# A two-layer attention and MLP kernel: loads of the ramp put later, ninth score blocks in shared units, a fourth bank pair for scores, and an instruction order found anew

## The chip, the core and the metric

The kernel runs on one core of a Trainium2 chip. The core has five engines with instruction streams of their own: TensorE (PE, with its weight loads shown apart as PEld), VectorE (DVE), ScalarE (ACT), GpSimd (POOL) and SyncE (SP), which here issues the DMAs. The metric is the device time of one execution in microseconds. The kernel before was run three times.

## The reference, cut to what matters

```python
def _A_ref(x, wqkv, wo):                 # B, S, D = 1, 2048, 576
    H = 32; Dh = D // H; W = 256         # 32 heads of 18
    q, k, v = split(x @ wqkv)
    scores = q k^T * Dh ** -0.5          # per head
    mask = (i - j >= 0) & (i - j < W)    # causal, sliding window of 256
    p = softmax(where(mask, scores, -1e9))
    return (p v) @ wo

def _B_ref(x, w1, b1, w2, b2):           # F = 4608
    y = layernorm(x)
    return gelu(y @ w1 + b1) @ w2 + b2

x = x + _A_ref(layernorm(x), wqkv, wo)
x = x + _B_ref(layernorm(x), w1, b1, w2, b2)
x = x + _A_ref(layernorm(x), wqkv, wo)
x = x + _B_ref(layernorm(x), w1, b1, w2, b2)
```

Both layers use the same weights. All tensors are bf16; the kernel keeps x in fp32.

## The kernel before, in words

**Tiles and chunks.** The 2048 rows are 16 tiles of 128. A chunk k is four tiles (512 rows) of one layer, so there are eight chunks; 0 and 4 are the first ones of their layers ("edge chunks"). A chunk goes through these stages, whose names the planner uses:
- layernorm and transposes: statistics on DVE (`ln_stats`, L696 and L700), 1/sqrt on POOL (`ln_rstd`, L709 and L711), normalized rows `xn` on DVE (L721), then a DMA transpose from SP into `xnTa` (L744). Chunk 0 is transposed on TensorE instead (L738) and copied by ACT (L741).
- `q<k>.<i>`: the q, k, v products of tile i with `wqkv`. Chunk 0 multiplies with the whole array (L800), chunk 1 with the whole array or in four column strips (L781, L784; function `quad`), later chunks with two half rows at once (L840). q and k are copied to `qn` (L861 on DVE, L858 on ACT), and transposed by DMA into `qT` and `kT` (L880); k of chunk 0 on TensorE (L874). Chunk 1's q goes to a free part of `x_res` and two of its k tiles to `xnTm`.
- `ea`, `eb`, `ec`: attention of head groups 0 to 2, 3 to 5, 6 and 7. A group is four heads, computed side by side in the array. `scores` makes one unit: up to 4 x 512 score columns (L909, four products of 32 rows at once), exp by ACT in two halves (L918), the masks by POOL (L939, affine_select). `pv` multiplies with v (L956), DVE transposes and divides (L967, L970, L973; the group's result is called `aq<g>`) and transposes into `attT` (L977).
- `t`: the product with `wo` (L781), the residual (L1019), layernorm, and DMA transposes into `xnTm` (L744; tile i's is called `xm<k%2>_<i>`).
- `ga`, `gb`, `gc`: a third each of the hidden layer, 12 x 128 columns, w1 in two half rows (L1076) and GELU by ACT (L1086); `ma`, `mb`, `mc`: the products with w2 (L781 wide or L784 in four strips), and the residual.

Stages of chunk k's attention, chunk k-1's MLP and chunk k+1's q, k, v are interleaved. Loads are issued on SP (L633): `xin_load` (x tiles), `w_load` (wqkv), `wo_load`, `w1_load` (a group of 768 columns in three DMAs), `w2_load` (half of a third each), and the biases. A list of names in `reads` makes a load wait for that work.

**Masks and units.** With a window of 256, a tile of keys meets three tiles of queries. A head group of an inner chunk has twelve 128 x 128 score blocks, three units of four. In an edge chunk it has nine, three units of three (`units_of`).

**The order.** Nothing is ordered by hand. Each step is a task with a cost, a latency and a priority; `Plan.schedule` simulates the five engines, the DMA queue and eight PSUM banks, always starts the task that can start first (ties by priority), and the resulting order of each engine is written out with semaphore waits. The table `PL.nudge` adds a number to the priorities of each stage. `place` chooses the PSUM banks: scores take two bank pairs out of `SC`, other products take banks out of `FILL` or `OUT`. `keep_warm` puts products on a tile of zeros (`warm`, L683) into pauses of TensorE that the simulation shows in the first 140 us. `SWITCH` is the cost that the planner gives to a change of tiling on TensorE (whole array, half rows, quarter rows, column strips).

Of the kernel before, what the change touches and what calls it, by code (L numbers as in the profile page):

```python
# [6 lines left out]
BF16 = mybir.dt.bfloat16  # L7
ACT = mybir.ActivationFunctionType
ALU = mybir.AluOpType
# [177 lines left out]
class Plan:  # L187
# [75 lines left out]
    def schedule(self):  # L263
# [9 lines left out]
        def place(t):  # L273
# [4 lines left out]
            for h in t.alloc:  # L278
                best = None
                for n, c in enumerate(h.choices):  # L280
                    bs = (c, c + 1) if h.pair else (c,)
                    if any(b in taken or b not in bank_free for b in bs):
                        continue
                    key = (max(bank_free[b] for b in bs), n)
                    if best is None or key < best[0]:
                        best = (key, c, bs)
# [14 lines left out]
        def starves(t, st, got):  # L301
# [4 lines left out]
            where, when = place(f)  # L306
# [12 lines left out]
        served = {}  # L319
        n = len(self.tasks)  # L320
        while len(order) < n:
            best = None
            cands = []
            for e in ENGS:
                for t in released[e]:
# [4 lines left out]
                    if t.alloc:  # L330
                        got, when = place(t)
                        if got is None:
                            continue
                        st = max(st, when)
# [30 lines left out]
            if t.dma is not None:  # L365
# [15 lines left out]
                done = at + t.move  # L381
                for o in served:
                    if o != t.eng and served[o] > at:
                        both = min(t.move, served[o] - at)
# [3 lines left out]
                q.append((done - t.move, done, t.desc))  # L388
# [42 lines left out]
SWITCH = 0.095  # L431
TURN_FROM = 40.0
# [4 lines left out]
def build_kernel(nc, A_x, A_wqkv, A_wo, B_x, B_w1, B_b1, B_w2, B_b2, out):  # L437
# [19 lines left out]
    PVG = [()] * 8  # L457
# [22 lines left out]
    PL.nudge = {"": -230.72, "b": 275.87, "ea0.0": 68.12, "ea0.2": -36.73, "ea0.p0": 25.27, "ea0.p1": 8.39, "ea0.p2": 19.16,  # L480
                "ea1.0": 48.8, "ea1.1": 0.92, "ea1.2": 10.77, "ea1.p0": 185.12, "ea1.p1": 14.37, "ea1.p2": 11.32, "ea2.0":
                -226.13, "ea2.1": 8.7, "ea2.2": 4.73, "ea2.p1": 11.09, "ea2.p2": -5.57, "ea3.0": -4.87, "ea3.1": -6.42,
                "ea3.2": 56.72, "ea3.p0": 54.64, "ea3.p1": -4.95, "ea3.p2": 4.43, "ea4.0": -157.3, "ea4.1": -50.05, "ea4.2":
                -2.47, "ea4.p0": -14.11, "ea4.p1": -7.45, "ea4.p2": -38.62, "ea5.0": 5.68, "ea5.1": 129.24, "ea5.2": 138.02,
                "ea5.p0": -17.5, "ea5.p1": -18.27, "ea5.p2": 7.12, "ea6.0": -10.43, "ea6.1": -81.59, "ea6.2": -13.37,
                "ea6.p0": 8.67, "ea6.p1": -3.19, "ea6.p2": -25.74, "ea7.0": -0.76, "ea7.1": 39.58, "ea7.2": 7.45, "ea7.p0":
                67.13, "ea7.p1": 7.91, "ea7.p2": 33.86, "eb0.3": 1.56, "eb0.4": -30.65, "eb0.p3": 18.78, "eb0.p4": -1.29,
                "eb0.p5": -0.92, "eb1.3": -271.59, "eb1.4": -222.31, "eb1.5": 1.61, "eb1.p3": -2.23, "eb1.p4": 24.61,
                "eb1.p5": 1.63, "eb2.4": -298.09, "eb2.5": 16.43, "eb2.p3": 10.4, "eb2.p4": 0.7, "eb2.p5": -1.71, "eb3.4":
                -25.34, "eb3.5": 25.11, "eb3.p3": 29.88, "eb3.p4": 58.63, "eb3.p5": -4.78, "eb4.3": -12.25, "eb4.4": -0.16,  # L490
                "eb4.p3": -72.79, "eb4.p4": -13.68, "eb4.p5": -18.7, "eb5.3": -43.09, "eb5.4": -75.21, "eb5.5": -69.51,
                "eb5.p3": 33.39, "eb5.p4": 14.38, "eb6.3": -211.52, "eb6.4": -50.12, "eb6.5": 3.59, "eb6.p3": 1.78, "eb6.p4":
                7.56, "eb6.p5": 43.58, "eb7.3": -2.1, "eb7.4": -56.17, "eb7.5": 15.09, "eb7.p3": 2.77, "eb7.p4": 32.12,
                "eb7.p5": -15.09, "ec0.6": -24.25, "ec0.7": -285.95, "ec0.p6": -298, "ec0.p7": -298, "ec1.6": -14.11,
                "ec1.7": -8.95, "ec1.p6": 69.38, "ec1.p7": -15.01, "ec2.6": -248.94, "ec2.7": -26.42, "ec2.p6": 6.89,
                "ec3.6": -23.39, "ec3.7": 0.06, "ec3.p6": 15.99, "ec4.6": -27.23, "ec4.7": -15.88, "ec4.p7": 22.38, "ec5.6":
                4.81, "ec5.7": -19.36, "ec5.p6": -21.13, "ec5.p7": 7.48, "ec6.6": -4.15, "ec6.7": 34.6, "ec6.p6": -48.38,
                "ec6.p7": -2.73, "ec7.6": -14.95, "ec7.7": -4.74, "ec7.p6": -5.14, "ec7.p7": -14.29, "ga0": 51.09, "ga0.0+":
                -221.62, "ga0.1": -34.97, "ga0.1+": 1.66, "ga0.2": 12.74, "ga1": -52.79, "ga1.0": 14.73, "ga1.0+": -300,
                "ga1.1": -3.67, "ga1.1+": -5.08, "ga1.2": 3.12, "ga1.2+": 8.05, "ga2": 10.11, "ga2.0": -4.37, "ga2.0+":  # L500
                -108.79, "ga2.1": -18.6, "ga2.1+": -20.12, "ga2.2": -0.27, "ga2.2+": -9.83, "ga3": -28.92, "ga3.0": -1.99,
                "ga3.0+": -171.06, "ga3.1": 72.56, "ga3.1+": 0.86, "ga3.2": 24.22, "ga3.2+": 1.1, "ga4": -8.01, "ga4.0":
                3.65, "ga4.0+": 144.48, "ga4.1": 0.92, "ga4.1+": 5.08, "ga4.2": 10.41, "ga4.2+": 3.79, "ga5": -23.08,
                "ga5.0": 7.67, "ga5.0+": -232.94, "ga5.1": -13.61, "ga5.1+": -10.37, "ga5.2": 256.63, "ga5.2+": -3.75,
                "ga6.0": 17.03, "ga6.0+": -293.18, "ga6.1": -136.59, "ga6.1+": -2.84, "ga6.2": -106.7, "ga6.2+": 36.79,
                "ga7": 32.17, "ga7.0": -6.85, "ga7.0+": -298.91, "ga7.1": -2.5, "ga7.1+": -295.12, "ga7.2": -50.23, "ga7.2+":
                -298.91, "gb0.0": 39.23, "gb0.0+": -201.39, "gb0.1": 7.33, "gb0.1+": -8.01, "gb0.2": 28.02, "gb0.2+": -54.76,
                "gb1": -5.04, "gb1.0": 125.3, "gb1.0+": -293.18, "gb1.1": 179.72, "gb1.1+": 20.59, "gb1.2": -5.13, "gb1.2+":
                10.15, "gb2": -28.5, "gb2.0+": -298.03, "gb2.1": 0.97, "gb2.1+": 2.45, "gb2.2": -34.25, "gb2.2+": -25.68,
                "gb3": 16.67, "gb3.0": 14, "gb3.0+": -193.69, "gb3.1": 300, "gb3.1+": 2.02, "gb3.2": -42.12, "gb3.2+": -7.63,  # L510
                "gb4": 2.01, "gb4.0": 6.64, "gb4.0+": 76.76, "gb4.1": 14.19, "gb4.1+": 47.56, "gb4.2": 281.48, "gb4.2+":
                -0.8, "gb5": -54.31, "gb5.0": 14.06, "gb5.0+": -283.84, "gb5.1": 0.7, "gb5.2": -2.79, "gb5.2+": 41.37, "gb6":
                28.29, "gb6.0": -15.34, "gb6.0+": -138.05, "gb6.1": 2.91, "gb6.1+": 5.18, "gb6.2": -56.75, "gb6.2+": 25.92,
                "gb7": -1.58, "gb7.0": -6.36, "gb7.0+": 214.45, "gb7.1": 27.22, "gb7.1+": -10.59, "gb7.2": -20.88, "gb7.2+":
                214.45, "gc0.0": 1.32, "gc0.0+": -285.07, "gc0.1": 9.39, "gc0.1+": -9.63, "gc0.2": -2.51, "gc0.2+": 10.94,
                "gc1": -5.22, "gc1.0": 18.43, "gc1.0+": -20.31, "gc1.1": 260.5, "gc1.1+": -2.2, "gc1.2": -6.34, "gc2": -3.11,
# [427 lines left out]
    def pv(k, g, units, bo, first, last, prio):  # L944
# [20 lines left out]
        if not last:  # L965
            return
# [349 lines left out]
```

## Time and profile before

| | |
|---|---|
| median of 3 runs | 865.6 us (865.04 to 865.78) |
| the profiled execution | 864.13 us |
| its span, first to last instruction | 862.3 us |
| busy PE, ACT, DVE, POOL | 848.7, 593.2, 392.0, 377.9 us |
| mean granted TensorE clock | 0.998 |
| moved by DMA | 119.77 MB, mean 139 GB/s |
| first products with wqkv | 7.56 us |
| first scores | 21.16 us |
| first products with w1 | 87.07 us |
| changes of tiling on TensorE | 415 |

An engine's busy time says how long it had an instruction in work; products on TensorE overlap, and a product's duration is longer than its distance to the next. So stretches of equal products are read from the chain of waits, which gives the length of a whole stretch. "Ramp" means the first 87 us, up to the first w1 products: chunk 0 and the start of chunk 1, when no MLP work is there to fill pauses.

### The profile page before, as it was taken

Reading aid. Unit: us, or ns where it says so; the run is one execution under the profiler, and the core shown is the slowest. Engines: PE = TensorE matmul, PEld = TensorE weight load, DVE = VectorE, ACT = ScalarE, POOL = GpSimd, SP = SyncE. Lnnn points to the kernel's source line nnn. Section 1 sums busy time; section 2 is a strip of 40 time slices with the busy share of each in tenths; the row PEclk is TensorE's granted clock in tenths of the full one; section 3 lists DMA queues with packets and bytes.
Section 4 is the critical chain, followed back from the end, with each engine's and each line's share of the span. In section 5 each row is a group of like instructions: output and inputs, shape, how many; then the busy total and the mean of one; then the engine's idle time right before and its main releaser. Section 6 shows DMA issues by size and latency. Waiting matters only on the chain.

```text
span 862.3 us, 26990 instructions
## 1 busy us (share of the span) xinstructions
PE 848.7 (98%) x11578; PEld 520.5 (60%) x11578; DVE 392.0 (45%) x934; ACT 593.2 (69%) x741; POOL 377.9 (44%) x560
## 2 busy tenths in 40 slices
PE   8899999999999999999999999999999999999998
PEld 6556556656556565565655655656556656656656
DVE  7689424655228542384424832655224434243012
ACT  4796788768667588573875876737787589771730
POOL 4687544465135653264421863425454276222100
PEclk9999999999999999999999999999999999999999
DMA  7887435351583615957359443673536953355320
GB/s 192 197 193 142 124 125 148 109 163 44 166 181 107 163 43 166 204 93 169 90 151 218 92 139 125 116 177 98 173 112 119 289 155 105 126 166 146 120 83 28
DMA packets 181862, 119.77 MB, mean 139 GB/s; under 512 B 107440, under 2 KB 181744, under 8 KB 181744
## 3 DMA queue, kind: packets, MB, share of 16 engines
q1 hardware_dynamic: 181744, 118.05, 53.7%
q8 instruction: 91, 1.49, 0.7%
q14 instruction: 27, 0.22, 0.1%
HBM read 90.10 MB, written 2.36 MB: 107 GB/s over the span
## 4 chain that ended last, share of the span: by engine, by line
PE 87%; DMA 4%; DVE 4%; ACT 2%; issue 2%; SPq 1%; POOL 1%; POOLq 0%; DVEq 0%; ACTq 0%
PE ps L1076 31%; PE ps L781 27%; PE ps L784 9%; PE ps L840 8%; PE ps L909 6%; PE ps L956 4%; ACT pT L918 2%; DMA xnTm<-xn 2%; PE ps L800 1%; DMA xnTa<-xn 1%; DVE x_res L1019 1%; DVE xn L721 1%; DVE st_all L696 1%; SPq L633 1%; DMA wqkv<-in_A_wqkv_dram 1%
## 5 line engine op out<-in xcount | busy, mean ns | idle before, releaser
L939 POOL TENSOR_SCALAR_AFFINE_SELECT pT<-pT 128x512 bf16<-128x512 bf16 (+1 forms) x368 | 282.8, 789 | 250.1 <-ACT pT L918 244.9
L918 ACT ACTIVATE pT<-ps 128x1024 bf16<-128x1024 f32 (+1 forms) x384 | 345.1, 974 | 58.0 <-PE ps L909 57.6
L1076 PE MATMUL ps<-xnTm,w_sb 64*128 64x512 bf16 x2592 | 290.5, 376 | 0.9 <-DVE x_res L1019 0.3
L1086 ACT ACTIVATE hT<-ps,b1col 128x512 bf16<-128x512 f32 x276 | 167.4, 687 | 173.9 <-PE ps L1076 173.4
L1076 PEld LDWEIGHTS ps<-xnTm,w_sb 64*128 64x128 bf16 x2592 | 128.8, 94 | 142.5 <-issue 6.4
L781 PE MATMUL ps<-w_sb,hT 128*128 128x288 bf16 x1506 | 201.1, 287 | 0.0
L1019 DVE TENSOR_TENSOR x_res<-ps,x_res 128x288 f32<-128x288 f32 x224 | 100.0, 450 | 188.2 <-PE ps L781 162.1
L781 PEld LDWEIGHTS ps<-w_sb,hT 128*128 128x128 bf16 x1506 | 139.9, 98 | 51.5 <-issue 15.6
L840 PE MATMUL ps<-wqkv,xnTa 64*128 64x288 bf16 x1296 | 91.7, 283 | 1.6 <-DVE x_res L1019 1.1
L967 DVE STREAM_TRANSPOSE oq<-ps 128x512 f32<-128x512 f32 x64 | 45.8, 716 | 98.9 <-PE ps L956 98.0
L784 PE MATMUL ps<-w_sb,hT 128*32 128x288 bf16 x2424 | 83.7, 287 | 0.1
L861 DVE CAST qn<-ps 128x288 bf16<-128x288 f32 x120 | 49.0, 450 | 76.4 <-PE ps L840 68.8
L840 PEld LDWEIGHTS ps<-wqkv,xnTa 64*128 64x128 bf16 x1296 | 61.3, 94 | 31.4 <-issue 2.7
L784 PEld LDWEIGHTS ps<-w_sb,hT 128*32 128x32 bf16 x2424 | 62.2, 97 | 13.6 <-issue 4.2
L909 PE MATMUL ps<-qT,kT 32*128 32x384 bf16 (+2 forms) x1216 | 64.1, 276 | 2.8 <-ACT pT L918 2.3
L696 DVE BATCH_NORM_STATS2 st_all<-x_res 128x6 f32<-128x288 f32 (+1 forms) x128 | 53.4, 442 | 6.7 <-DMA x_res<-in_A_x_dram 5.8
L709 POOL TENSOR_SCALAR vtmp<-mv_all 128x1 f32<-128x1 f32 (+1 forms) x43 | 8.8, 204 | 107.7 <-DVE mv_all L700 105.3
L848 DVE CAST vA<-ps 128x288 bf16<-128x288 f32 x64 | 26.5, 450 | 63.2 <-PE ps L840 59.5
L1092 POOL TENSOR_TENSOR x_res<-x_res,b2bc 128x576 f32<-128x576 f32 x32 | 40.2, 1275 | 32.8 <-ACT hT L1086 32.8
L956 PE MATMUL ps<-pT,vA 128*20 128x384 bf16 (+2 forms) x1408 | 50.5, 276 | 0.2 <-DVE qn L861 0.2
L909 PEld LDWEIGHTS ps<-qT,kT 32*128 32x128 bf16 x1216 | 19.4, 92 | 42.8 <-issue 26.3
L781 PE MATMUL ps<-wo_sb,attT 128*128 128x288 bf16 x320 | 42.1, 287 | 0.3 <-DVE qn L861 0.3
(56 smaller groups left out, 465.1 us busy)
## 6 DMA issues: line engine op xcount, KB each, us to landing
w_sb<-in_B_w_dram SPq DMA_DIRECT2D x46, 864.0 KB, 6.0
w_sb<-in_B_w_dram SPq DMA_DIRECT2D x48, 768.0 KB, 4.7
w_sb<-in_B_w_dram SPq DMA_DIRECT2D x96, 48.0 KB, 4.4
wqkv<-in_A_wqkv_dram SPq DMA_DIRECT2D x3, 576.0 KB, 5.6
x_res<-in_A_x_dram SPq DMA_DIRECT2D x3, 576.0 KB, 5.7
wqkv<-in_B_w_dram SPq DMA_DIRECT2D x2, 864.0 KB, 6.3
out_dram<-x_res SPq DMA_DIRECT2D x12, 144.0 KB, 2.0
wo_sb<-in_A_wo_dram SPq DMA_DIRECT2D x4, 144.0 KB, 2.6
```

The source lines that it names most:

```text
L696: add("dve", lambda e, i=i, s=s: e.bn_stats(st_all[:, t, i, :], s[:, t, i * HB:(i + 1) * HB]), reads=res, writes=[f"st{t}_{i}"], cost=0.37 ...
L781: return e.matmul(bank(b)[:, 0:HB], lhs, rhs, start=start, stop=stop, skip_group_check=True)
L784: ins = e.matmul(bank(b)[32 * j:32 * j + 32, 0:HB], lhs[:, 32 * j:32 * j + 32], rhs, start=start, stop=stop, tile_position=(0, 32 * j), sk ...
L840: ins = e.matmul(bank(bs[o])[:, 0:HB], xnTa[r:r + 64, c, i * 128:(i + 1) * 128], wqkv[r:r + 64, c, col:col + HB], start=(c == 4), stop=(ph ...
L861: add("dve", lambda e, b=bs[o], dst=dst: e.tensor_copy(dst, heads_of(bank(b))), reads=[bs[o]], writes=[f"qn{sl}h{o}"], cost=0.375, lat=0.1 ...
L909: ins = e.matmul(two(bs[j // 2])[:, j % 2, col:col + nq * 128], k_of(T0 + so)[0][32 * j:32 * j + 32, g, :], qs[32 * j:32 * j + 32, g, qo * ...
L918: add("act", lambda e, h2=h2: e.activation(pT[:, sl, 2 * h2:2 * h2 + 2, lo:hi], two(bs[h2])[:, :, lo:hi], ACT.Exp, scale=SCALE), reads=[bs ...
L939: add("pool", lambda e, ap=ap, pat=pat, sgn=sgn, kind=kind: e.affine_select(ap, ap, pattern=pat, compare_op=(ALU.is_ge if kind == "d" else ...
L956: ins = e.matmul(bank(bo)[32 * j:32 * j + VW, qo * 128:(qo + nq) * 128], vA[:, (T0 + so) % VS, 8 * j + g, :], pT[:, sl, j, col:col + nq * ...
L1019: add("dve", lambda e: e.tensor_tensor(x_res[:, t, sl], bank(b)[:, 0:HB], x_old[:, t, sl], ALU.add), reads=[b] + ([f"xin{t}"] if first els ...
L1076: ins = e.matmul(bank(bks[i])[:, 0:n], w1_sb[r:r + 64, sls[i], col:col + 128], xnTm[r:r + 64, k % 2, c, 0:n], start=(c == 4), stop=(ph == ...
L1086: add("act", lambda e, ff=ff, hd=hd, bk=bk: e.activation(hd[:, 0:n], bank(bk)[:, 0:n], ACT.Gelu_apprx_tanh, bias=b1col[:, ff:ff + 1]), rea ...
```

## The change

- Loads. `b1` and `b2` wait for `aq5` of chunk 0 (before: for `k3`), x tiles 8 to 11 for `aq1` (before: `v1h0`), `wo` for `aq2` (`aq0`). Of the first three w1 groups one waits for `aq3`, one for `aq5`, one for `xm0_0` (before: `k3`, `v0h0`, `aq2`). The two halves of the first third of w2 wait for `xm0_2` and `xm0_3` (before: `aq5`, `aq7`). x tiles 12 to 15 wait for chunk 1's `aq2` (before: `xm0_3`).
- Start. x tiles 1 and 2 to 3 are loaded from ACT's queue, behind the table load; `vtmp` of the first four tiles is computed on DVE; tile 0's second copy of its last columns comes from DVE, its five transposes go to two banks, and DVE copies two of the five. q products of tile 0 wait for their own half of the weights.
- Units of edge chunks. Per group: two units of four blocks, and a ninth block that shares a unit with the ninths of the other groups of the stage. Chunk 0's first stage has three units of three blocks, three of four, one of four (two blocks each of two groups) and one of two. The function `E0` is gone, and `E` makes all orders.
- Banks. `SC` has a fourth pair (6, 7). `place` treats all banks that are free at the time as equally good and takes the first in the list (before: the one that was free longest).
- Planner. Other latencies for DMA transposes and loads, 0.8 us more for a large load after a transpose (`TURN_DMA`), and another `PL.nudge` (some 280 numbers).

In the order that results, SP issues after x tiles 4 to 7: four transposes for q, four for `xnTa`, two q and two k of chunk 1, x tiles 8 to 11, and then the others. 59 products on the warm tile stand where 34 stood. Fourteen score units use the pair (6, 7).

The diff, cut to its core (the nudge table is left out):

```diff
-        def place(t):
+        def place(t, now):
...
-                    key = (max(bank_free[b] for b in bs), n)
+                    key = (max(now, max(bank_free[b] for b in bs)), n)
...
+                mv = t.move + (TURN_DMA if t.desc >= 500 and t.dma != "t" and turned.get(t.eng) and served.get(t.eng, 0.0) >= at else 0.0)
+                turned[t.eng] = t.dma == "t"
...
-    SC = (0, 2, 4)
+    SC = (0, 2, 4, 6)
...
-    xin_load(1, 1)
     w_load(0)
-    xin_load(2, 2)
     w_load(1)
     w_load(2)
+    table("exp", -10)
+    xin_load(1, 1, q="act", prio=-9)
+    xin_load(2, 2, q="act", prio=-8)
...
-        add("pool", lambda e: e.tensor_scalar(vtmp[:, t0:t0 + n], var, sc, bi, op0=ALU.mult, op1=ALU.add),
+        add("dve" if t0 < 4 and not fused else "pool", lambda e: e.tensor_scalar(vtmp[:, t0:t0 + n], var, sc, bi, op0=ALU.mult, op1=ALU.add),
...
-            b = Bank(FILL)
-
-            for cs in ((0, 1, 2, 3), (4,)):
+            bs = [Bank(FILL)] * 2 if i else [Bank(FILL), Bank(FILL)]
+            groups = ((0, 1, 2, 3), (4,)) if i else ((0, 1, 2), (3, 4))
...
-            reads=rd, writes=[f"{dname}{i}"] + ..., dma="t", ring=8, cost=1.3, lat=0.7, move=1.0, desc=640, prio=prio)
+            reads=rd, writes=[f"{dname}{i}"] + ..., dma="t", ring=8, cost=1.3, lat=0.95, move=0.75, desc=640, prio=prio)
...
-        if t0 == 0:
-            us = [[(0, 0, 3, 0)], [(1, 1, 3, 128)], [(2, 2, 2, 256), (3, 3, 1, 128)]]
...
+        if CH[k][1]:
+            seq = [on(g, *u) for g in gs for u in units_of(k)]
+        elif k == 0 and gs[0] == 0:
+            seq = [on(g, (0, 0, 3, 0)) for g in gs]
+            bs = [on(g, (1, 1, 3, 0), (2, 2, 1, 384)) for g in gs]
+            cs = [on(g, (2, 3, 1, 256 * n), (3, 3, 1, 256 * n + 128)) for g, n in ((0, 0), (1, 1), (2, 0))]
+            seq += [bs[0], cs[0] + cs[1], bs[1], bs[2], cs[2]]
+        else:
+            seq = []
+            for g in gs:
+                seq += [on(g, (0, 0, 3, 0), (2, 2, 1, 384)), on(g, (1, 1, 3, 0), (2, 3, 1, 384))]
+            seq.insert(2, [(g, 3, 3, 1, 128 * n) for n, g in enumerate(gs)])
...
-    dma("sp", b1in, ..., reads=["k3"], writes=["b1i"], cls="b", ring=2,
+        dma("sp", b1in, ..., reads=["aq5"], writes=["b1i"], cls="b", ring=2,
...
-    xin_load(8, 4, ["v1h0"], -4)
+                xin_load(8, 4, ["aq1"], -4)
...
-                w1_load(-1, ["k3"])
+                w1_load(-1, ["xm0_0"])
...
-            w2_load(0, 1, ("aq5", "aq7"))
+            w2_load(0, 1, ("xm0_2", "xm0_3"))
...
-                w1_load(-1, ["v0h0"])
-                w1_load(-1, ["aq2"])
+                w1_load(-1, ["aq3"])
+                biases()
+                PL.stage = "le0"
+                w1_load(-1, ["aq5"])
...
-                xin_load(12, 4, ["xm0_3"], 0)
+                xin_load(12, 4, ["aq2"], 3)
```

A unit's parts are (group, key tile, first query tile, query tiles, first column).

## The prediction

> **What bounds the kernel now.** I read the page's first part, then a table by stage, then the chain of waits, then the timelines of the ramp.
>
> ```profile
> span 862.3 us, 26990 instructions
> ...
> PE 848.7 (98%) x11578; PEld 520.5 (60%) x11578; DVE 392.0 (45%) x934; ACT 593.2 (69%) x741; POOL 377.9 (44%) x560
> ```
>
> TensorE is busy 98% of the span, so only fewer or better packed products on it, or the few places where it stands, can move the end. The table by stage, cut at the first score products (21.2), at 62.4 and at the first products with w1 (87.07), shows where it stands (columns: length, then busy time of PE, PEld, DVE, ACT, POOL, each with its count, then granted clock, DMA share, GB/s):
>
> ```profile
> 0.00:21.20 21.20, 18.09 (x158) 13.53 (x158) 15.30 (x46) 10.08 (x18) 9.45 (x28) 1.00 0.78 191
> 21.20:62.40 41.20, 36.75 (x543) 21.62 (x544) 29.22 (x71) 36.51 (x52) 29.64 (x45) 0.96 0.86 193
> 62.40:87.07 24.67, 23.75 (x372) 15.07 (x367) 23.39 (x59) 16.90 (x18) 17.78 (x30) 1.00 0.80 150
> 87.07:862.30 775.23, 770.07 (x10516) 470.23 (x10516) 324.11 (x759) 529.70 (x655) 321.00 (x458) 1.00 0.51 134
> ```
>
> After 87.07 PE stands 5 of 775 us; before it, 8.5 of 87, and only there does the granted clock fall. The chain of waits says on what (start, length, what):
>
> ```profile
> 22.36 4.98 DMA qT<-qn
> 27.70 4.74 DMA xnTa<-xn
> 32.48 2.59 PE ps L784 x40
> ```
>
> The fourth q transpose and the chunk-1 xnTa transposes took 4.7 to 5.0 us to land; xnTm's median on the page is 2.6. SP's timeline shows what stood between them, and ACT's what the delay did:
>
> ```profile
> 23.70 2.02 SPq L744 DMA_TRANSPOSE xnTa<-xn  x1
> 25.77 0.58 SPq L633 DMA_DIRECT2D b2bc<-in_B_b_dram  x1
> 26.45 2.52 SPq L744 DMA_TRANSPOSE xnTa<-xn  x2
> 29.02 0.57 SPq L633 DMA_DIRECT2D w_sb<-in_B_w_dram  x1
> ```
> ```profile
> 29.85 2.92 ACT L918 ACTIVATE pT<-ps 128x768 bf16<-128x768 f32 x4 [0.56 <-PE ps L909]
> 35.95 23.16 ACT L918 ACTIVATE pT<-ps 128x768 bf16<-128x768 f32 x32 [3.18 <-PE ps L909]
> ```
>
> PE's last scores before the hole end at 29.8, its next product starts at 32.48 when xnTa lands: 2.7 us. In 21.0 to 36.0 the granted clock averages 0.89, that is 15 x 0.11 / 0.5 = 3.3 us at half speed, and 40 quarter products (ten whole ones) take 2.59 us there against 1.3. ACT then starves 3.2 us and afterwards runs 23 us without a pause: chunk 0's exps are its bound.
>
> **Part 1: the loads of the ramp.** b1, b2, x tiles 8 to 11, two w1 groups (L633) leave the gap between the transposes; in the built order the four q and four xnTa transposes follow each other at SP's 1.24 us each, with only x tiles 4 to 7 ahead. That removes the 2.7 us hole and, of the half clock, the 32.48 to 35.0 when PE worked: 2.5 / 2 = 1.25. Sum -4.0. The moved loads now wait on attention groups (aq1 to aq5) and on xm0; SP issues in order, so the transposes of chunk 1's k and chunk 2's xn stand behind those waits. Cover: their first reader comes after all of chunk 0's scores, some 30 us later; without it, a late x8 load costs its own landing, 5.7 us. Bias and wo loads are read only in the tail and the first GELU. I cost them at 0 (bounds -0.5, +3).
>
> **Part 2: the start.** x1 to x3 are issued by ACT (after its 1.28 us table load), vtmp moves from POOL (0.19) to DVE, tile 0's transposes are split in two banks. This shortens tile 0's chain by about 0.3 us. But the first products waited 1.15 us for wq (7.56), the k products for wk (10.26); weights arrive by bytes, and these do not change. 0.0 (bounds -0.5, +0.5: x2-3 landed half a us after wq, and may now land before it). The order puts 70 instead of 80 q, k, v products ahead of the first scores; at 0.1225 (below) scores start 1.2 us earlier, near 20.0, and these 1.2 us of work are done later: no change of PE's sum, but ACT gets its exps sooner.
>
> **Part 3: switches.** PE pays when products of another tiling follow:
>
> ```profile
> 337.10 3.05 PE ps L781 x24
> ...
> 340.48 1.58 PE ps L781 x12
> ```
>
> Twelve products more cost 1.47, so one costs 0.1225 and an interruption 1.58 - 1.47 = 0.11. Counted in the order of the built kernels, changes of tiling fall from 415 to 402: 68 to 64 before the first w1 products, 347 to 338 after. So -0.4 in the ramp, -1.0 after it.
>
> **Part 4: ninth blocks.** Edge chunks 0 and 4 have nine 128-column score blocks per head group. Three units of three become two of four, and the ninths share units. Exps go from 384 to 366. Back to back, x32 of 768 columns take 23.16, 0.724 each, and 1024 columns 0.94 to 0.97, so a fixed part is near 0.07: 18 x 0.07 = 1.3 us less ACT, of which 0.6 in the ramp. PE streams the same columns in 64 more score and 64 more pv instructions, four abreast: 32 more sets. A pv row of four sets takes 0.67 for nine blocks, so sets overlap; bounds 0 and 32 x 0.16 = 5.1 (0.16 is what a lone set adds). I take 0.01 each, the low end, since the sets follow within one group: +0.3. POOL's selects (+8) stay below ACT.
>
> **Part 5: bank pairs, place, found order.** 14 score units take pair 6, all after the ramp, where PE stands 5 us of 775. Gain at most those; cost unknown where scores now take the fillers' banks 6 and 7: bounds -2, +2, taken at +0.2.
>
> **The ramp's sum.** From 21.16 to 87.07 PE had 200 whole products (24.5), 216 half ones at 2.20 / 36 (13.2), 204 score and pv blocks at 0.057 (11.6), nine transposes (0.5), 68 switches (7.5): 57.3 of 65.9. Of the missing 8.6, 4.0 are the hole; 4.6 are many waits of 0.2 to 0.5, mostly for ACT. After: 210 products and 64 switches, 58.1. The order adds 24 products on the warm tile (`keep_warm`), 24 x 0.107 = 2.6 us, in six places of this stretch: free where PE would wait for ACT anyhow, all on the path where not; taken at 0.2, since they stand before score units. So 20.0 + 58.1 + 4.6 + 0.2 = 82.9 against 87.07: -4.2. Bounds: 0 (next paragraph), and -7.2 if ACT never starves: 35.7 us of exps and copies from 20.4 on end at 56.1 instead of 62.2, and PE has 1.1 less behind them (36 half products fewer, nine pv blocks and six fillers more).
>
> Total: -4.2 - 1.0 + 0.3 + 0.2 = -4.7. The profiled execution took 864.13 (span 862.3 and 1.8 around it), 1.5 below the median of 865.6; the difference carries over: span 857.6, execution 859.4, median 860.9. About 0.2% (1.7 us) is the least that a measurement here can tell from no change.
>
> **Rivals.** *DVE takes over.* Between the first pv result (35.68) and chunk 0's last attq, DVE's work by rows grows from 27.2 to 32.6 us, since x8 to x11's statistics (8 x 0.44, 4 x 0.20) move in; it is busy 82% of 36 to 60 already, and the last attq releases the wo products. If DVE becomes the bound the 5.4 us eat the 4.2: 865.1. For: DVE 23.4 of 24.7 in the next stage. Against: it has pauses up to 35.
>
> *SP's head of queue, slower.* w2's first half no longer comes at 57.8; it waits on the landing of xm0_2, ahead of the transposes of xm0_0 and xm0_3, which the first w1 products need. From xm0_2's issue: landing 3.0, w2 0.4, two issues of 1.24, landing 5.5 beside a load (xnTa's largest) is 11.4; before, the same step took 6.1 (80.52 to 86.61). Before, these products started 0.5 us after the last landing, so +5.3 comes onto the path, and the pause brings the half clock, 1.7: 860.9 + 7.0 = 867.9. It decides when chunk 2's products left after the wo products (near 11.5 us) are used up. Against: the four wo tiles now run in one go, so that filler comes after them. The Trainium skill ("TensorE: Matmul & The Clock Gate", Part 1) halves the clock only after a whole idle window of about 3.4 us; here 2.7 us of standing was enough, so the trace decides. By that rule this rival would lose its 1.7 only if the pause stayed short.
>
> *The x tiles delay wq.* On a queue of their own they take turns with wq, which lands with them, up to 0.9 us later, and the first scores with it: 861.8. For: x2-3's landing kept DVE waiting 1.82 at 7.96, in the same half microsecond in which wq came. Against: k waits for wk anyway. The Trainium skill ("DMA: Bandwidth & Descriptors", Rules for kernel authors) says that spreading DMAs over issuing engines brings no bandwidth, since all share the 16 engines, and saves only issue time; by it part 2 gains nothing, and the sum above holds no gain for it either.
>
> *More.* With ACT fed early the small waits shrink too: ramp -7.2, 857.9.
>
> **Numbers.** Forecast 860.9 (858.9 to 863.0): 0.56. More, 857.9: 0.13. Late wq, 861.8: 0.08. DVE, 865.1: 0.13. Head of queue, 867.9: 0.10. Faster by over 0.2% 0.77, within 0.13, slower 0.10. The range 856.5 to 865.7 holds all but the last and the tails.
>
> **What would show it.** Right: the first w1 products near 83; no load between the q and xnTa transposes, these landing in 3 to 4 us; ACT's exps without the 3.2 us pause; clock 1.00 from 21 to 36; 402 changes of tiling and PE's idle after the ramp still near 5 us. Wrong: PE standing before the first w1 products for xnTm (head of queue); wo products waiting on DVE while ACT idles; first q products after 8.5; or new waits on w1 or w2 loads later on.

## The result, and the profile after

| | before | after |
|---|---|---|
| median beside each other | 865.32 us (863.8 to 865.78, 4 runs) | 873.06 us (869.51 to 874.29, 4 runs) |
| ratio, 95% interval | | 1.0087 (1.0064 to 1.0110) |
| the profiled execution, its span | 864.13, 862.3 us | 874.29, 872.6 us |
| first scores | 21.16 us | 19.41 us |
| first products with w1 | 87.07 us | 87.33 us |
| from there to the end of the span | 775.2 us | 785.3 us |

The forecast was 860.9 us with a range of 856.5 to 865.7, faster. The kernel became slower by 0.9%. The page of the kernel after, its span and busy times:

```profile
span 872.6 us, 27687 instructions
...
PE 854.2 (98%) x11950; PEld 524.3 (60%) x11950; DVE 390.6 (45%) x941; ACT 590.8 (68%) x722; POOL 379.1 (43%) x563
```

The table by stage, cut as before at the first scores, at 62.4 and at the first products with w1 (length, busy time of PE, PEld, DVE, ACT, POOL, granted clock, DMA share, GB/s):

```profile
0.00:19.45 19.45, 17.48 (x149) 12.78 (x149) 14.68 (x48) 9.12 (x17) 7.79 (x21) 1.00 0.81 204
19.45:62.40 42.95, 41.39 (x735) 26.18 (x738) 32.38 (x81) 36.52 (x45) 32.84 (x55) 1.00 0.77 144
62.40:87.33 24.93, 21.15 (x328) 12.88 (x315) 22.11 (x57) 16.65 (x18) 16.81 (x28) 0.99 0.82 148
87.33:872.60 785.27, 774.16 (x10754) 472.42 (x10754) 321.46 (x757) 528.47 (x645) 321.63 (x460) 1.00 0.52 135
```

The second row is what the prediction promised: PE stands 1.6 of 43 us there instead of 4.5 of 41, at full clock. The third row takes it back: PE stands 3.8 of 24.9 us instead of 0.9 of 24.7. In the fourth PE stands 11.1 us instead of 5.2. PE's list of waits in the whole execution says for what (us in all, times, longest):

```profile
PE ps L801 <- DVE qn L883: 2.3, 2, 2.0
PE ps L1095 <- DMA xnTm<-xn: 2.0, 1, 2.0
PE ps L929 <- DMA kT<-qn: 1.8, 2, 1.6
PE ps L862 <- DMA xnTa<-xn: 1.6, 2, 1.2
```

The first place is the ramp's end. SP's timeline, then the piece of the chain of waits that ends there, then PE's:

```profile
79.23 0.38 SPq L636 DMA_DIRECT2D w_sb<-in_B_w_dram  x1
79.74 3.15 SPq L764 DMA_TRANSPOSE xnTm<-xn  x2
```
```profile
81.70 5.39 DMA xnTm<-xn
```
```profile
84.98 0.40 PE L929 MATMUL ps<-x_res,kT 32*128 32x256 bf16 x8
87.33 4.94 PE L1095 MATMUL ps<-xnTm,w_sb 64*128 64x512 bf16 x30 [1.95 <-DMA xnTm<-xn]
```

w2's first load (864 KB) is issued just ahead of the last two xnTm transposes, and the last of them takes 5.39 us instead of the 2.58 of before. PE stands 1.95 us, and then 30 products take 4.94 us, since the clock is half from 87.04 to 90.45. The second place is the passage to chunk 2. DVE's timeline, then PE's:

```profile
177.70 0.43 DVE L732 TENSOR_SCALAR xn<-x_res,mv_all,rstd 128x576 bf16<-128x576 bf16 x1 [2.32 <-DMA xnTm<-xn]
...
178.70 1.54 DVE L883 CAST qn<-ps 128x288 bf16<-128x288 f32 x4
```
```profile
179.21 3.06 PE L801 MATMUL ps<-w_sb,hT 128*128 128x288 bf16 x12 [1.97 <-DVE qn L883]
```

DVE's next normalized rows want one of the four `xn` buffers, and a transpose still reads it (issued 173.06, landed 177.24). Behind it in DVE's order stand the four casts of q and k that free PE's banks. PE stands 1.97 us and the clock halves again (179.20 to 182.61: twelve products in 3.06 us, 1.64 at full clock).

### The profile page after: what moved, and what is told of

The parts are those of the page before. It is cut to its first block, busy times and chain, and to the rows that moved or that the text cites. A ratio compares the mean times of both kernels' runs of the same rounds, so it can differ in the third digit from the quotient of the medians.

```text
span 872.6 us, 27687 instructions
## 1 busy us (share of the span) xinstructions
PE 854.2 (98%) x11950; PEld 524.3 (60%) x11950; DVE 390.6 (45%) x941; ACT 590.8 (68%) x722; POOL 379.1 (43%) x563
## 3 DMA queue, kind: packets, MB, share of 16 engines
q8 instruction: 94, 1.54, 0.7%
## 4 chain that ended last, share of the span: by engine, by line
PE 85%; DMA 6%; DVE 2%; ACT 2%; issue 2%; POOL 2%; SPq 1%; DVEq 0%; POOLq 0%
PE ps L1095 31%; PE ps L801 27%; PE ps L804 9%; PE ps L862 8%; PE ps L929 6%; PE ps L982 4%; DMA xnTm<-xn 2%; ACT pT L940 2%; POOL pT L961 1%; DMA x_res<-in_A_x_dram 1%; DMA kT<-qn 1%; DVE st_all L707 1%; DMA xnTa<-xn 1%; DMA wqkv<-in_A_wqkv_dram 1%; DVE qn L883 0%
## 5 line engine op out<-in xcount | busy, mean ns | idle before, releaser
L961 POOL TENSOR_SCALAR_AFFINE_SELECT pT<-pT 128x512 bf16<-128x512 bf16 (+2 forms) x376 | 283.5, 778 | 276.6 <-ACT pT L940 259.7
L940 ACT ACTIVATE pT<-ps 128x1024 bf16<-128x1024 f32 (+2 forms) x366 | 342.8, 1014 | 63.0 <-PE ps L929 62.6
L801 PE MATMUL ps<-w_sb,hT 128*128 128x288 bf16 x1458 | 197.5, 288 | 2.3 <-DVE qn L883 2.3
L801 PEld LDWEIGHTS ps<-w_sb,hT 128*128 128x128 bf16 x1458 | 135.1, 98 | 55.0 <-issue 17.2
L804 PE MATMUL ps<-w_sb,hT 128*32 128x288 bf16 x2616 | 89.4, 286 | 0.3 <-DVE x_res L1038 0.2
L804 PEld LDWEIGHTS ps<-w_sb,hT 128*32 128x32 bf16 x2616 | 67.9, 97 | 14.3 <-issue 4.0
L929 PE MATMUL ps<-qT,kT 32*128 32x128 bf16 (+2 forms) x1280 | 62.6, 271 | 3.8 <-DMA kT<-qn 1.8
L801 PE MATMUL ps<-wo_sb,attT 128*128 128x288 bf16 x310 | 40.3, 286 | 0.0
L732 DVE TENSOR_SCALAR xn<-x_res,mv_all,rstd 128x576 bf16<-128x576 f32 (+1 forms) x64 | 35.7, 580 | 9.7 <-DMA xnTm<-xn 7.5
```

The source lines that it names most:

```text
L801: return e.matmul(bank(b)[:, 0:HB], lhs, rhs, start=start, stop=stop, skip_group_check=True)
L804: ins = e.matmul(bank(b)[32 * j:32 * j + 32, 0:HB], lhs[:, 32 * j:32 * j + 32], rhs, start=start, stop=stop, tile_position=(0, 32 * j), sk ...
L929: ins = e.matmul(two(bs[j // 2])[:, j % 2, col:col + nq * 128], k_of(T0 + so)[0][32 * j:32 * j + 32, g, :], qs[32 * j:32 * j + 32, g, qo * ...
L940: add("act", lambda e, h2=h2: e.activation(pT[:, sl, 2 * h2:2 * h2 + 2, lo:hi], two(bs[h2])[:, :, lo:hi], ACT.Exp, scale=SCALE), reads=[bs ...
L961: add("pool", lambda e, ap=ap, pat=pat, sgn=sgn, kind=kind: e.affine_select(ap, ap, pattern=pat, compare_op=(ALU.is_ge if kind == "d" else ...
```

## The experiments

In all of them the order of every engine is kept as the planner found it, and single tasks are put elsewhere in it, by this function behind the sort in `Plan.schedule` (cut; n counts from 0):

```python
def moved(order):   # MOVES: (engine, first name written, n-th such task), and the one it goes behind
    for what, behind in MOVES:
        a = order.pop(nth(*what))
        order.insert(nth(*behind) + 1, a)
    return order
```

The ratios are to runs of the kernel before on the same chip. The mean granted clock of a run tells how many stretches of half clock it holds, since one (3.41 us) lowers it by 0.002; where it matters, medians of the runs at 1.000 stand beside. Times of first products and waits are of one execution of each kernel, the profiled one.

**e1: w2's first load behind the transposes** (on the kernel after).

```diff
+MOVES = (("sp","w2s0",0) behind ("sp","q1",1))
```

> The kernel after, with every engine's order kept, but the first load of w2 (the half that waits for the landing of xm0_2) issued on SP behind the transposes of xm0_0 and xm0_3 and the q transpose after them, instead of ahead of them. Theory A (the loads' place in SP's list gave the ramp's gain back): the last two xnTm transposes land 2.6 to 3.2 us after their issue, as they do in both kernels where no load stands ahead, instead of 6.77 and 5.39; they are there by 84.6, before TensorE has done its last scores (85.38), so the 1.95 us of standing go, and with them the half clock of 87.04 to 90.45, which cost the first w1 products 1.5 us: 873.1 - 3.4 = 869.7, first w1 products near 85.5. Rival B (the transposes are late because of the bytes that are under way at that time, not because of the queue's order, or TensorE waits for something else there too): landings stay over 4.5 us and the time within 1 us of 873.1. Rival C (the stretch is not on the path: what is won is waited for a few us later, since w2's half now lands near 89): first w1 products near 85.5, but the median stays within 1 us of 873.1.

Ratio 1.0078 (1.0050 to 1.0106), no clear difference to after's. The last transpose landed in 2.58 us, but PE now lost time earlier: it stood 1.71 us for the bias load (`hT`), the clock halved, and the first w1 products came at 88.3. The run could not tell the theories apart; it pointed to a third place.

```profile
65.48 0.19 PE L1208 MATMUL ps<-ident,hT 36*128 36x36 bf16 x1 [1.71 <-DMA hT<-in_B_b_dram]
...
66.67 3.90 PE L862 MATMUL ps<-wqkv,xnTa 64*128 64x288 bf16 x36 [0.67 <-DVE oq L991]
```

**e2: the passage at 176 to 197** (on after).

```diff
+MOVES = (("dve","xn2",5), with its copy (POOL) and transpose (SP), behind ("dve","qn1h1",2)),
+        (("sp","w2s0",3), ("sp","w2s1",3) behind ("sp","xa3",2))
```

> The kernel after with two edits at the passage from chunk 1 to chunk 2 (176 to 197 us), and nothing else moved: VectorE's normalisation of chunk 3's third tile (which stood 2.32 us at 177.70, waiting for a buffer of xn that a transpose still read) with its copy and its transpose goes behind the four casts of qn that stood behind it; and the two loads of w2 that SP issues at 186.2 and 187.0 go behind the transpose of chunk 3's fourth tile. Theory A (of the 10 us that the kernel after loses from its first w1 products on, half lies here, in one queue place on VectorE and one on SP): TensorE's 1.97 us of standing at 179.2 go, the half clock of 179.2 to 182.6 with its 1.4 us, and the 1.18 us at 196.06: 873.1 - 4.6 = 868.5. Rival B (only the place moves: TensorE waits there for another thing, VectorE's sums or the scores): the time stays within 1 us of 873.1, with a pause of over 1.5 us still between 176 and 200.

Ratio 1.0056 (1.0035 to 1.0077), 2.2 to 2.7 us below after's two ratios (1.0082 and 1.0087), with intervals that overlap; at a clock of 1.000 the median is 867.7 (5 runs), against 869.4 for after (2 runs of g3, on another chip). The pause is gone. Theory A, at about half its size: the pause at 179 is not in every execution of after (g3).

**e3: both.** 

> Both edits in one kernel. If each gain is on the path and they do not share it: 873.1 - 3.4 - 4.6 = 865.1, the time of the kernel before within its measurement. If what was lost in the first place is the cause of the second (a stretch that starts late and stays late), the sum is less: about the larger of the two alone, 868.5.

Ratio 1.0040 (1.0024 to 1.0055): the median is lower than of either alone, and short of before. PE at the second place, timeline:

```profile
175.50 0.40 PE L929 MATMUL ps<-qT,kT 32*128 32x256 bf16 x8
175.83 1.64 PE L801 MATMUL ps<-w_sb,hT 128*128 128x288 bf16 x12
```

**e4: the load of w2 put in front, in the kernel before.** This is the opposite test.

```diff
+MOVES = (("sp","w2s0",0) behind ("sp","xm0_3",0))      # before.py: between the xnTm transposes
```

> The kernel before, with one thing done as after: the first load of w2 (864 KB by its shape on the page, there issued at 57.8) stands on SP between the second and the third of chunk 0's xnTm transposes, at 81.8. Theory A: the third and fourth transpose land 5 to 7 us after their issue instead of 3.46 and 2.58, the first w1 products start near 89.5 instead of 87.07, TensorE stands about 2.5 us there and its clock halves behind it, another 1.5: 865.3 + 4.0 = 869.3. Rival B (the queue's order does not matter): within 1 us of 865.3, or below it, since the load no longer stands among the transposes of 57 to 66.

Ratio 1.0052 (1.0033 to 1.0072), 4.5 us: theory A, to half a us, and with the first w1 products at the time that it named. PE's timeline:

```profile
85.13 1.51 PE L840 MATMUL ps<-wqkv,xnTa 64*128 64x288 bf16 x18
89.51 4.24 PE L1076 MATMUL ps<-xnTm,w_sb 64*128 64x512 bf16 x22 [2.86 <-DMA xnTm<-xn]
```

So moving one load of 864 KB in front of two transposes costs 4.5 us; this needs nothing else of the change.

**f1: the loads of 43 to 70 out of the transposes there** (on after).

```diff
+MOVES = (("sp","b1i",0) behind ("sp","woB3",0)),
+        (two w1 groups and ("sp","b2",0) behind ("sp","q3",1))
```

> The kernel after, with every engine's order kept but SP's between 43 and 70 us: the bias load b1 goes behind the wo loads (before the four xnTa transposes, with no attention group to wait for), and the two groups of w1 and b2 go behind the last q transpose of that stretch, so that no load stands among the transposes of 50 to 70 us. Theory A (the loads that the change moved out of 20 to 35 us jam the same queue again at 48 to 70): in the traces of the kernels run so far TensorE stood 0.4 to 2.3 us at 56 to 59 for xnTa and 1.1 to 1.9 at 63.5 to 65.5, for the bias load or for ACT behind it; these go, 2.5 us in the middle: 873.1 - 2.5 = 870.6, if the load of w2 at 79 doesn't take them back. Rival B (the stretch ends where xnTm lands, whatever comes earlier): 873.1 within 1 us. Rival C (w1's first group, now landing near 76 to 80, comes too late): TensorE stands for w1 at its first products, 874 or more.

Ratio 1.0138 (1.0115 to 1.0162). Rival B and more: the wait for the bias went and the xnTa transposes landed in 2.6 to 3.2 us, but the first w1 products still came at 87.41. All that was won was waited for at w2's place, and every run had two or three stretches of half clock (0.996 and 0.994), against none to two in after's runs.

```profile
87.41 1.04 PE L1095 MATMUL ps<-xnTm,w_sb 64*128 64x512 bf16 x4 [2.75 <-DMA xnTm<-xn]
```

**g2: both ramp edits, f1's and e1's.** 

> The kernel after with the ramp's two edits together (the loads of 48 to 70 behind the transposes there, w2's first load behind xnTm's) and nothing at 176 and 680. Moving the first loads alone gave a ratio of 1.0138, moving w2 alone 1.0078. Theory A (two loads' places in series: the first gain is only seen once the second is free): first w1 products near 84.8, no half clock there, and the ratio falls by 2.5 + 1.5 us of 865 from after's, to about 1.004. If the pause at 177, which hangs on a transpose landing in 4.4 instead of 2.6 us, comes with it, the ratio is nearer 1.006; without it, nearer 1.002.

Ratio 1.0055 (1.0035 to 1.0075), 7.2 us below f1. The first w1 products came at 85.06 at full clock. The two places stand in series: what the first wins shows only when the second is free.

**f2: f1's, e1's and e2's edits.** 

> All three edits: the loads of 48 to 70 behind the transposes, w2's first load behind xnTm's, and the two edits at 176 to 197. Two of them together gave 867.7. Theory A (the places add up): 867.7 - 2.5 = 865.2, and the first w1 products near 84. If the ramp is bound by something else than the loads (VectorE's chain of normalisations, ACT's exps), the first w1 products stay near 86.5 and the time at 867.7.

Ratio 1.0028 (1.0017 to 1.0039); first w1 products at 84.71, right behind the last scores:

```profile
84.37 0.40 PE L929 MATMUL ps<-x_res,kT 32*128 32x256 bf16 x8
84.71 1.66 PE L1095 MATMUL ps<-xnTm,w_sb 64*128 64x512 bf16 x12
```

**f3: and the k transpose at 687.** In after PE stood 1.56 us for it, behind a w1 group and a load of w2.

```diff
+        (("sp","w2x0",0) and the w1 group of ("sp","w1a1",12) behind ("sp","k5",4))
```

> The three edits, and a fourth at 676 to 690 us: the last k transpose of the last chunk, for which TensorE stood 1.6 to 2.0 us in the kernel after and in the three built from it, goes ahead of two loads of w2's last half and a group of w1. Theory A: that pause goes: 865.2 - 1.9 = 863.3, below the kernel before (864.75 in the last runs). Rival B (two loads of w2 issued still earlier hold the queue's engines all the same): the k transpose lands less than 1 us sooner, and the time stays within 1 us of the kernel with three edits.

Ratio 1.0011 (0.9999 to 1.0024): close to the kernel before's time, not below it. No run of the twelve had half clock, while 10 of before's 23 had; at 1.000 the medians are 864.6 and, for before, 862.8 (13 runs), so 1.8 us are still lost there. The k transpose landed 3.15 us after its issue, against 5.39 in f2. PE's timeline at the fourth place:

```profile
681.15 3.86 PE L804 MATMUL ps<-w_sb,hT 128*32 128x288 bf16 x120
685.28 0.40 PE L929 MATMUL ps<-qT,kT 32*128 32x384 bf16 x8 [0.27 <-issue]
```

**f4: products on the warm tile ahead of the first w1 products** (on after, one execution).

```diff
+    order.insert(i, 16 products on `warm`)      # i: the first product of ga0.0
```

> The kernel after with one thing added: 16 products on the warm tile (1.7 us at 0.107 each) directly ahead of the first w1 products, into a bank that is free there, so that TensorE is busy while it waits for xnTm; nothing else moves. If the half clock of 87.04 to 90.45 comes from the standing of 1.95 us before it, the clock stays at 1.00 there, the first 108 products with w1 take 11.9 us instead of 13.3, and the wait itself stays: 1.4 us less from the first w1 products to the end. If it comes from something else (the kind of products that start there), it stays halved.

The clock stayed 1.00 there and 18 w1 products took 2.12 us, while xnTm still landed 4.9 to 6.6 us after its issue. So in this execution the half clock goes with the standing, not with the kind of product. How much it costs cannot be read from this run, whose ramp was disturbed earlier (half clock at 67.96).

**g3: the kernel after again.** 

> The kernel after, unchanged, beside the others on this chip: how far its time goes from run to run. By four runs it is 869.5 to 874.3, ratio 1.0087. If the pauses of about 2 us at 56 to 66, 85 to 87, 177 to 179 and 691 to 693 each come with or without a half clock, the runs spread by 1.5 us for each and the median stays within 1.007 to 1.011.

Ratio 1.0082 (1.0069 to 1.0095). Its profiled execution has no pause at 179; instead PE stood for the bias at 65 and the clock was half from 65.10 to 71.92. The places are the same ones, but which of them strike differs from run to run.

**g1: the prediction's Part 1 alone, in the kernel before.**

```diff
+MOVES = (two w1 groups and ("sp","b2",0) behind ("sp","xa2",0))   # before.py: out of 19 to 33
```

> The kernel before, with only what Part 1 of the prediction called the gain: the two groups of w1 and b2 (seven loads that SP issues at 19.4 to 32.6 among the transposes) go behind the last of the four xnTa transposes; every other order stays, x tiles 8 to 11 and b1 too. Theory A (the prediction's sum for the hole was right, and what gave it back in the kernel after were the places to which it moved the loads): the q and xnTa transposes land in 2.6 to 3.5 us, the hole at 29.8 to 32.5 and the half clock behind it go, the first w1 products start near 83, and the kernel is 4 us faster than before, ratio 0.995. Rival B (what follows the ramp's first part is bound by VectorE's chain and ACT's exps, so that the hole was filled with waiting in any case): the hole goes, but the first w1 products start at 86 to 87 and the ratio is 0.999 to 1.000. Rival C (the loads now stand among the transposes of chunk 1's q and k at 35 to 45): a wait of 2 us or more at 40 to 60, and no gain.

Ratio 1.0005 (0.9990 to 1.0020). The wait for xnTa in the hole is gone and 40 products at 30.90 take 1.41 us instead of 2.59, but two new waits for DVE stand 10 us later, 2.07 us together, the first behind a q transpose: rival C, at half its size. PE's timeline, then DVE's:

```profile
30.90 1.41 PE L784 MATMUL ps<-wqkv,xnTa 128*32 128x288 bf16 x40
...
41.03 0.67 PE L956 MATMUL ps<-pT,vA 128*20 128x384 bf16 x16 [1.12 <-DVE qn L861]
...
42.92 0.79 PE L781 MATMUL ps<-wqkv,xnTa 128*128 128x288 bf16 x5 [0.95 <-DVE qn L861]
```
```profile
40.42 0.46 DVE L861 CAST qn<-ps 128x288 bf16<-128x288 f32 x1 [1.73 <-DMA x_res<-qn]
```

**h1: all loads that nothing reads yet out of the ramp, in the kernel before.**

```diff
+MOVES = (two w1 groups and b2 behind ("sp","q1",1)), (w2s0, w2s1, third w1 group behind ("sp","q3",1))
```

> The kernel before, with all loads that nothing reads before the first w1 products taken out of 19 to 67 us on SP: two groups of w1 and b2 behind a q transpose near 70, w2's two loads and the third w1 group behind the last q transpose, near 86.6; every other order as before. Moving only the first of them by 10 us removed the hole at 30 and gave it all back at 39 to 43, where VectorE waited 1.73 us for a q transpose behind them (ratio 1.0005). Theory A (what was missing was a place with room in the queue): no wait of over 1 us between 21 and 85, the first w1 products near 83, ratio 0.9955. Rival B (ACT's exps bound the ramp once it is fed: 36.5 us of work in 21 to 62, and 23 us of them without a pause): the first w1 products come 1 to 2 us sooner, 85 to 86, ratio 0.998 to 0.999. Rival C (w2's loads now land near 92 and 97, w1's third group near 100, and are missed): a pause at 98 to 110, ratio 1.000 or more.

Ratio 1.0025 (1.0013 to 1.0037). In the profiled execution the first w1 products came 1.8 us sooner, and then x tiles 12 to 15, behind w2, were late: DVE stood 12.4 us for them, PE 2.0 for DVE, and the clock halved. Rival C had a pause at this time, but for w2 and w1; none of the three had named this wait.

```profile
97.61 1.18 DVE L696 BATCH_NORM_STATS2 st_all<-x_res 128x6 f32<-128x288 bf16 x3 [12.40 <-DMA x_res<-in_A_x_dram]
```

**h2: as h1, with the last three loads behind the x load.** 

> The kernel before with the loads of 19 to 67 us moved as in the last run (two w1 groups and b2 near 68, w2's two loads and the third w1 group near 86), but these last three behind the load of x tiles 12 to 15 instead of ahead of it. In the last run the first w1 products came 1.8 us sooner than before, and then VectorE stood 12.4 us for that x load (landed 97.58 instead of 90.95), TensorE 2.0 us for VectorE at 101.7, and the clock halved. Theory A (that was the whole loss): no pause at 95 to 102, and the 1.8 us stay: ratio 0.998, the ramp's loads in their right places worth 1.8 us, not 4. Rival B (w2's loads, 5 us later still, are missed at 98): a pause of 2 us there for w2, ratio 1.002.

Ratio 0.9999 (0.9986 to 1.0012). The pause at 100 is gone, and nothing is gained. At a clock of 1.000 the medians are 862.7 (9 runs) and 862.4 for before (12 runs).

**h3: only the first move of h1.** 

> The kernel before with only the two w1 groups and b2 moved from 19 to 33 us to near 68, w2's loads and the third w1 group left at 49 to 67. The same move by 10 us gave ratio 1.0005. Theory A (the places add up along the queue): the hole at 30 and the pause at 39 to 43 go, and the five loads at 67 to 72, with w2's second load just ahead of them, delay chunk 0's xnTm transposes, so that part of the 1.8 us comes back at 83: first w1 products 85.5 to 87, ratio 0.998 to 1.000. If the first w1 products come at 83 or earlier, VectorE's chain was not the bound there and the prediction's 4.2 were right.

Ratio 1.0002 (0.9987 to 1.0017); at 1.000, 862.7 (7 runs). The first w1 products came at 85.12: neither theory A's 85.5 or later nor the 83 that would have borne out the prediction. They waited 1.35 us for an xnTm transpose. Three ways to move the loads out of the hole, and no gain from any. None of the versions beats the kernel before.

## Why the prediction was wrong, by its own steps

The forecast wanted 4.7 us less, and the kernel takes 7.3 more (0.85% of 863, the mean of its two ratios). Of these 12 us the runs put about 7.4 into Part 5, the found order, which was priced at +0.2: 2.3 and 1.5 for two places, and 3.6 that f2 and f3 still take too long from the first w1 products on. About 4.3 lie in the ramp: 2.3 for the moved loads, priced at 0, and 2.0 that f2 and f3 still lack of first w1 products at 82.9, where the hole was to give its gain. The parts are differences of medians and of single executions, so they are rough.

- **Part 1, the hole, -4.0.** The loads left the stretch as described (scores at 19.41 against 20.0 forecast, clock 1.00, ACT's pause of 3.18 shrunk to 1.28). But the sum took 2.7 us of standing as won, and read the hole as one wait. PE's timeline of before has a product in it:

```profile
30.72 0.34 PE L909 MATMUL ps<-qT,kT 32*128 32x384 bf16 x4 [0.91 <-ACT pT L918]
32.48 2.59 PE L784 MATMUL ps<-wqkv,xnTa 128*32 128x288 bf16 x40 [1.42 <-DMA xnTa<-xn]
```

  Only 1.42 us are a wait for a late transpose. The 0.91 ahead of it are a wait for ACT, and they stay in g1, h2 and h3. What is won at 30 is in part waited for again: in g1 at 41 to 43 for DVE, which waits for a q transpose; ahead of the first w1 products in h2 for DVE and in h3 for an xnTm transpose. Of h2, then of h3:

```profile
30.58 0.34 PE L909 MATMUL ps<-qT,kT 32*128 32x384 bf16 x4 [0.91 <-ACT pT L918]
...
85.35 4.92 PE L1076 MATMUL ps<-xnTm,w_sb 64*128 64x512 bf16 x44 [0.82 <-DVE vA L848]
```
```profile
82.25 1.51 PE L840 MATMUL ps<-wqkv,xnTa 64*128 64x288 bf16 x18
85.12 3.20 PE L1076 MATMUL ps<-xnTm,w_sb 64*128 64x512 bf16 x28 [1.35 <-DMA xnTm<-xn]
```

  From the first scores to the first w1 products PE stands 5.4 us in before, and still 6.0 in g1, 4.7 in h2 and 4.9 in h3. The medians of the three show no difference to before; their intervals leave a gain of at most 1.2 us. How long the hole is in before's runs without half clock stays open: the two traces that have it, before and e4, both have half clock behind it.

  The 1.25 for the half clock was counted once for every run. By the runs' clocks, before holds a stretch of it in about half of its runs, wherever it lies (11 of 23 beside h2: 12 runs at 1.000, 9 at 0.998, 2 at 0.996), and h2 and h3, which lack the wait, still in 3 of 12 and 4 of 11. It costs more than was counted: before's medians are 862.4, 864.3 and 866.0, so 1.6 to 1.9 us each. The execution on which the sum was made had one.
- **Part 1, the moved loads, 0 (bounds -0.5, +3).** The transposes behind the loads were not followed to who waits for them, and one first reader was overlooked: the PE product that transposes b1 stands in the ramp, and PE stood 1.7 to 2.0 us for b1 in e1, e2 and g3. g2 against g3, on one chip, puts the two ramp places at 0.27% (2.3 us, intervals overlapping). In series they hide each other: by the ratios, w2's place is worth less than 1 us when it is undone alone (e1), and 7.2 once the other is undone (f1, then g2).
- **The fillers, 0.2.** The ramp's sum took 24 more products on the warm tile as nearly free. In f2, with every place of the ramp undone and the clock at 1.00, the way from the first scores to the first w1 products is 65.7 us, against 62.9 forecast and 63.9 in h2, which has the kernel before's products. PE stands 3.2 us there instead of 4.7, but is busy for 62.6 instead of 59.2; the warm products are 3.5 of that, and ten products that moved behind the first scores some 1.2. So f2's first w1 products come only 0.6 us sooner than h2's. No run leaves the warm products out, so it isn't shown how many of them lie on the path.
- **The rival "SP's head of queue"** (0.10) names the mechanism, the load, the two transposes and the half clock; e4 shows it in the kernel before. The sign that it named, PE standing for xnTm before the first w1 products, is in the profile of after. Its price of 7.0 was made on first w1 products at 82.9; PE's own work reached to 85.4 in after, so it stood 1.95, not 5.3, and e4's 4.5 is nearer than 7.0. "Against: filler comes after the wo tiles" was right on the filler and wrong that it covers the wait.
- **"DVE takes over"** was right in so far as DVE holds PE ahead of the first w1 products in h2; but that is the kernel before's order, without the moved statistics. What these cost in after, no run tests.
- **Part 5, the found order, +0.2 (bounds -2, +2).** This is the largest error. Two places of the new order cost more than the bound together. For the passage at 179, three comparisons (after to e2, e1 to e3, g2 to f2) give 2.3 to 3.3 us by the ratios, the same way each time, though in each the intervals overlap. For the k transpose at 687, f3 against f2 gives 1.5 us (0.0017, intervals overlapping), and PE's standing there falls from 1.08 to 0.27. Beyond them, f2 and f3 still take 778.4 and 778.3 us from the first w1 products to the end, against 775.2 before and 774.7 forecast. PE stands 7.2 and 7.0 us in this stretch instead of 5.1, in small waits (in f2 1.08 at 685 and 0.47 at 181, in f3 1.12 at 291 for an xnTa transpose), and its work is 1.1 us longer. These were not undone one by one: about 3 us of the order stay open.
- **Parts 2 to 4** (start 0.0, switches -1.4, ninth blocks +0.3) are small beside this. ACT's busy time fell by 2.4 (593.2 to 590.8; 1.3 forecast). PE's, by the trace of f3, is 851.3 against 848.7, and the 25 more products on the warm tile are in it. No run tests the switches alone, so their gain isn't shown.
- **The clock.** That a pause of some 2 us can halve the clock held; that it does was taken as certain. The stretches of half clock lie on a grid: in after they begin at 87.04 and 179.20, 27 times 3.413 us apart. In these traces PE's busy time in one stretch of the grid, at full clock, goes with the clock of the next. The table by windows, of after, then of e3:

```profile
175.79:179.20 3.41, 1.45 (x28) 0.78 (x22) 1.50 (x6) 2.71 (x3) 0.85 (x3) 1.00 0.33 50
179.20:182.61 3.41, 3.40 (x20) 1.78 (x20) 1.35 (x4) 0.03 (x1) 3.10 (x5) 0.50 0.24 48
```
```profile
685.73:689.15 3.42, 1.65 (x43) 1.09 (x36) 0.82 (x2) 1.28 (x3) 1.69 (x2) 1.00 1.11 209
689.15:692.56 3.41, 3.41 (x35) 2.40 (x33) 2.91 (x9) 2.46 (x3) 1.65 (x2) 1.00 0.97 337
```

  With 0.55 to 1.55 us of work in a stretch (eleven of them, in seven traces) the next was half; with 1.69 or more it was not; between 1.61 and 1.68 both were seen: about half of the window. Once half, the clock was full again after one stretch, except in g3, where it took two. A pause that the grid's line cuts in two brought no half clock (2.02 us up to 690.38 in e2, cut at 689.27). The Trainium skill ("TensorE: Matmul & The Clock Gate", Part 1) tells of such a window, free-running and 3.413 us long; the grid agrees. It puts the drop after a whole idle window; here half of one is enough, and the traces decide.

Together: the four places undone leave 1.0 of the 7.3 us (f3), or 1.8 between runs at a clock of 1.000. So where the loss came from is shown for the most part. That the hole alone gives no gain is shown; where its gain goes is read from single executions, and about 3 us of the order stay open.

## What to carry to other kernels

A load that leaves a jam joins another: for its new place, list each transfer behind it in the queue and who waits for that, and price it with a landing behind a load (here 4.5 to 6.8 us against 2.6). Before a pause is priced, look for products inside it: each part of it has its own cause. A pause is worth only what the stages behind it don't give back, and the cheap test is to take it away alone in the old kernel, before the rest is built on it. Where pauses of 2 us halve the clock in some runs and not in others, compare runs of the same granted clock.

## What the runs showed of the hardware that was not expected

**Transposes land late while program loads are under way.** The pause at 179 hangs on two transposes that landed in 4.40 and 4.18 us with no load ahead of them. The DMA list of after from 168.5 to 173.1 us (queue, packets, MB, share of 16 engines):

```profile
q1 hardware_dynamic: 1344, 0.33, 58.6%
q8 instruction: 1, 0.02, 1.4%
issues: line engine op xcount, KB each, median us to landing
xnTm<-xn SPq DMA_TRANSPOSE x2, 4.3
```

One packet of a queue of the kind "instruction" lies among them (16 KB at 170.93, and the next at 175.24, beside the second transpose). In the traces of all sixteen runs I took the xnTa and xnTm transposes before whose issue (or at most 0.6 us after it) all earlier transfers had landed, and asked whether an instruction packet was under way between 1.25 us after the issue and the landing. Without one the 190 of them landed in 2.54 to 2.83 us; with one, the 135 took 2.55 to 4.70, and 66 more than 3.8. The Trainium skill ("Runtime: NRT & Kernel Launch", Instruction fetch mechanics) says that instructions come in blocks of 16 KiB through a DMA queue, mostly hidden; the page of after has 94 packets of 1.54 MB on one such queue, 16 KB each, and by this count they are not hidden from a transpose. The Trainium skill ("DMA: Bandwidth & Descriptors", Queues, rings and completion order) has a reason that would fit: the signal of completion lands only after every earlier write of that DMA engine, across its queues. No run here took the packets away, so the cause is argued from the count, not shown by an experiment.
